# Dealing the rows of the first x tiles, meant to let a DMA engine read them in sequence

## The chip, the core and the metric

The kernel runs on one core of one Trainium2 chip. The metric is the device time of one execution in microseconds (us); medians of several executions are quoted. A ratio is the mean time of one kernel's runs over that of the other's of the same rounds, so it is not quite the ratio of the medians quoted beside it.

Engines: PE is TensorE, PEld its weight loads, DVE VectorE, ACT ScalarE, POOL GpSimd; SP only issues DMAs here ("SPq" is its queue).

## The reference

```python
B, S, Dm, Df = 1, 2048, 1024, 3584          # bf16 inputs
g = jnp.einsum("bsd,df->bsf", x, w_gate)
u = jnp.einsum("bsd,df->bsf", x, w_up)
h = gelu_tanh(g) * u
return jnp.einsum("bsf,fd->bsd", h, w_down)
```

## The kernel before

The kernel works in two passes (`ip`) of 1024 rows of x, each of two halves (`c`) of 512 rows, with a recursive matrix product that needs fewer multiplications. All of this is unchanged. What matters is the very beginning. The first 512 rows come as four tiles of 128 rows, are transposed by PE, and only then can the first product with the weights start. The other x blocks come by DMA transposes.

```python
    def store(ip, c, i, dc, put):
        st = slot([P, N], bf16, "st")
        put(st)
        r0 = (2 * ip + c) * N + i * P
        nc.sync.dma_start(out=out2[r0 : r0 + P, dc * N : (dc + 1) * N], in_=st)
    ...
    def load_x(c):
        t = []
        for i in range(NS):                       # four tiles, 256 KB each
            xn = slot([P, Dm], bf16, "xn")
            r0 = c * N + i * P
            nc.sync.dma_start(out=xn, in_=x2[r0 : r0 + P, :])
            t.append(xn)
        return t
    ...
    xT = new_x()
    xn0 = load_x(0)
    wf = wpool.tile([P, 2, NKB, 2 * P], bf16, name="w")
    for k0, k1 in ((0, 2), (2, 5), (5, NKB)):
        load_wf(nc.sync, k0, k1)                  # the first weights
    w = load_w(1)
    for ko in range(NKB):
        transposing(xT, 1, ko, N)                 # second half of x, by DMA transpose
    ...
        keep_warm(NWARM, N)
        for i in range(NS):
            if i == 2:
                keep_warm(2, 2 * P)
            turn(xT, xn0, 0, i)                   # PE transposes of tile i
        plain(bank[0:4], 0, range(0, 2), parts=2) # first products with weights
```

## Time and profile before

| what | value |
|---|---|
| time, median of 3 runs (6 by the time of the result) | 539.86 us (540.15) |
| lowest and highest of these 6 | 539.61, 540.94 |
| PE busy | 534.1 of 538.8 us |
| PE's last unbroken stretch | 7.91 to 535.68 us |
| last of the four x tiles landed | 6.99 us |

The page of the kernel before gives the span, the busy time of PE and the chain of work that ended last.

```profile
span 538.8 us, 7447 instructions
...
PE 534.1 (99%) x2409; PEld 381.2 (71%) x2409; DVE 341.5 (63%) x524; ACT 261.4 (49%) x463; POOL 238.5 (44%) x215
...
PE 98%; DMA 1%; SPq 0%; ACT 0%; issue 0%
```

The chain of waits in order of time, kernel before (start in us, length in us, what):

```profile
2.12 4.87 DMA xn<-in_x_dram
6.99 0.05 issue
7.04 0.62 PE bank L447 x8
7.66 0.22 PE bank L111 x2
7.88 0.03 issue
7.91 527.77 PE bank L111 x2366
```

From 7.91 to 535.68 us the chain is PE and nothing else; a last store of the output follows. Whatever starts that stretch earlier or later moves the end by the same amount, as long as nothing new makes PE wait. The 4.87 us of DMA ahead of it are the loads that the change touches.

The view of the tile `xn`, kernel before. The SPq line has the duration of one issue on SP (least, median, most, in ns); the last line is the time from issue to landing.

```profile
L440 SPq DMA_DIRECT2D xn<-in_x_dram x4: 392/420/432, 0.7 to 2.1; - x4
...
  PEld L447: 1.8, 3
...
DMA to landing us min/median/max: 2.8/3.8/4.9
```

The trace also records every DMA packet and, on the semaphore of each load, 16 completions, read here as one for each of the 16 DMA engines that the profile counts. The first x is 512 packets of 2 KB.

### The profile page before, as it was taken

The numbers are of one execution on the slowest core, as the hardware profiler recorded it, in microseconds if no ns is written. First come the engines' busy times: TensorE is split into PE (matmuls) and PEld (weight loads), VectorE is DVE, ScalarE is ACT, GpSimd is POOL, SyncE is SP. The second block draws the span as 40 slices with busy tenths as digits, with TensorE's granted clock in tenths as the row PEclk, the third lists the DMA queues.
The fourth block names the chain that finished last, engine by engine and source line by source line (L and its number), as shares of the span: only waits on it lengthen the run. The fifth ranks groups of instructions, "written<-read, shape, count | busy, mean of one in ns | idle before, by whom it ended". The sixth has DMA issues, their size and how long they took to land.

```text
span 538.8 us, 7447 instructions
## 1 busy us (share of the span) xinstructions
PE 534.1 (99%) x2409; PEld 381.2 (71%) x2409; DVE 341.5 (63%) x524; ACT 261.4 (49%) x463; POOL 238.5 (44%) x215
## 2 busy tenths in 40 slices
PE   8999999999999999999999999999999999999997
PEld 5568686867677746888867677676868685488886
DVE  2986766767676894694955455555554649676730
ACT  2556675766666410255355555555555551114431
POOL 1179966677773500000097767676766600000000
DMA  9675656749472999989872223242420049573751
GB/s 243 157 185 168 185 176 175 220 133 260 131 235 72 381 366 297 307 192 296 238 195 80 78 80 88 70 118 63 133 71 9 2 147 390 184 236 96 237 181 51
DMA packets 108198, 93.29 MB, mean 173 GB/s; under 512 B 17280, under 2 KB 93056, under 8 KB 108160
## 3 DMA queue, kind: packets, MB, share of 16 engines
q1 hardware_dynamic: 108160, 92.82, 59.4%
q8 instruction: 19, 0.31, 0.3%
q14 instruction: 19, 0.16, 0.1%
HBM read 74.45 MB, written 15.20 MB: 166 GB/s over the span
## 4 chain that ended last, share of the span: by engine, by line
PE 98%; DMA 1%; SPq 0%; ACT 0%; issue 0%
PE bank L111 98%; DMA xn<-in_x_dram 1%; SPq L440 0%; PE bank L447 0%; ACT st L412 0%
## 5 line engine op out<-in xcount | busy, mean ns | idle before, releaser
L93 POOL TENSOR_TENSOR s<-w 128x512 fp32r<-128x512 bf16 x102 | 119.2, 1189 | 163.2 <-DVE t L90 86.0
L111 PE MATMUL bank<-t,s 128*128 128x512 f32 x648 | 151.7, 390 | 0.0
L111 PEld LDWEIGHTS bank<-t,s 128*128 128x128 f32 x648 | 121.6, 188 | 25.5
L111 PE MATMUL bank<-xT,w 128*128 128x512 bf16 (+1 forms) x504 | 109.7, 376 | 0.0
L107 ACT COPY p<-bank 128x512 f32<-128x512 f32 x124 | 69.9, 590 | 45.4 <-PE bank L111 44.9
L111 PEld LDWEIGHTS <-w 128*128 128x128 bf16 x504 | 48.1, 98 | 58.1 <-issue 3.4
L90 DVE TENSOR_TENSOR hT<-g,bank 128x512 bf16<-128x512 f32 x112 | 76.8, 687 | 17.5 <-PE bank L111 4.5
L90 DVE TENSOR_TENSOR sum<-bank,p 128x512 f32<-128x512 f32 x54 | 37.3, 691 | 79.5 <-PE bank L111 78.4
L179 ACT ACTIVATE g<-sum 128x512 f32<-128x512 f32 x81 | 51.4, 635 | 74.5 <-DVE sum L90 74.2
L111 PE MATMUL bank<-q 128*128 128x512 f32 x240 | 58.9, 389 | 0.0
L93 POOL TENSOR_TENSOR s<-w,s 128x512 fp32r<-128x512 bf16 x50 | 57.7, 1176 | 0.0
L93 POOL TENSOR_TENSOR s<-s,w 128x512 fp32r<-128x512 f32 x50 | 57.2, 1165 | 0.0
L111 PE MATMUL bank<-t,sa 128*128 128x512 f32 x216 | 55.9, 401 | 0.0
L111 PE MATMUL bank<-tb,s 128*128 128x512 f32 x216 | 53.3, 389 | 0.0
L107 ACT COPY u<-bank 128x512 f32<-128x512 f32 x62 | 35.5, 589 | 33.5 <-PE bank L111 33.2
L111 PEld LDWEIGHTS bank<-q 128*128 128x128 f32 x240 | 45.0, 188 | 9.4
L111 PE MATMUL bank<-raw,hT 128*128 128x512 bf16 x224 | 48.7, 379 | 0.0
L102 ACT CAST tb<-raw 128x512 fp32r<-128x512 bf16 x28 | 17.3, 626 | 62.1 <-PE bank L111 27.6
L111 PEld LDWEIGHTS bank<-t,sa 128*128 128x128 f32 x216 | 40.6, 188 | 9.5
L111 PEld LDWEIGHTS bank<-tb,s 128*128 128x128 f32 x216 | 40.5, 188 | 8.4
L90 DVE TENSOR_TENSOR bank<-bank,p 128x512 f32<-128x512 f32 x54 | 37.7, 699 | 8.8 <-PE bank L111 6.2
L90 DVE TENSOR_TENSOR q<-hT 128x512 fp32r<-128x512 bf16 x56 | 38.4, 685 | 4.3 <-PE bank L111 4.3
(44 smaller groups left out, 442.1 us busy)
## 6 DMA issues: line engine op xcount, KB each, us to landing
raw<-in_w_down_dram SPq DMA_DIRECT2D x76, 256.0 KB, 5.0
q<-td SPq DMA_DIRECT2D x60, 256.0 KB, 5.1
w<-in_w_gate_dram SPq DMA_DIRECT2D x27, 512.0 KB, 5.9
w<-in_w_up_dram SPq DMA_DIRECT2D x27, 512.0 KB, 7.0
td<-m SPq DMA_DIRECT2D x12, 768.0 KB, 4.5
w<-td SPq DMA_DIRECT2D x6, 1024.0 KB, 10.0
out_dram<-st SPq DMA_DIRECT2D x32, 128.0 KB, 1.7
td<-w SPq DMA_DIRECT2D x2, 768.0 KB, 6.2
```

What stands on the lines that cost most here:

```text
L90: nc.vector.tensor_tensor(out=out, in0=a, in1=b, op=op)
L93: nc.gpsimd.tensor_tensor(out=out, in0=a, in1=b, op=op)
L102: nc.scalar.copy(out=t, in_=src)
L107: nc.scalar.copy(out=t, in_=ps)
L111: nc.tensor.matmul(ps, lhsT=lhs, rhs=rhs, start=start, stop=stop, skip_group_check=True)
L179: nc.scalar.activation(g, src, ACT.Gelu_apprx_tanh)
```

## The change

The intent: over the four tiles each DMA engine should read 64 KB in sequence, eight rows (16 KB) per tile, and not jump 256 KB from tile to tile. 64 KB is 1 MB in 16 equal shares. Row 32e + 8i + j goes to partition 8e + j of tile i. The columns of that half of x are then permuted through both products, and the stores of these rows put them back.

```diff
+    def dealt(rows, i):
+        return rows[:N].rearrange("(e i j) d -> i e j d", i=NS, j=8)[i]
+
     def store(ip, c, i, dc, put):
         st = slot([P, N], bf16, "st")
         put(st)
         r0 = (2 * ip + c) * N + i * P
-        nc.sync.dma_start(out=out2[r0 : r0 + P, dc * N : (dc + 1) * N], in_=st)
+        to = out2[:, dc * N : (dc + 1) * N]
+        to = dealt(to, i) if ip == c == 0 else to[r0 : r0 + P]
+        nc.sync.dma_start(out=to, in_=st)
 ...
             xn = slot([P, Dm], bf16, "xn")
-            r0 = c * N + i * P
-            nc.sync.dma_start(out=xn, in_=x2[r0 : r0 + P, :])
+            nc.sync.dma_start(out=xn, in_=dealt(x2, i))
```

## The prediction

> What bounds the kernel. The page's busy table has PE at 534.1 of 538.8 us (99%). The chain of work that ended last is 98% PE matmuls: from 7.91 us to 535.68 us it is PE without a break (527.77 us). Ahead stand 0.67 us of start, 1.45 us in which SP issues the four loads of the first x, 4.87 us of DMA until the last of them lands at 6.99 us, and 0.84 us of transposes and first matmuls. The change touches these 4.87 us, about 1% of the span, and eight of 32 output stores (128 KB, landing in 1.7 us by the DMA view), which nothing in the chain waits for.
>
> What the change does. Bytes, packets (2 KB rows) and issues stay the same. Before, each 256 KB tile is one contiguous stretch[...]. The columns of the c = 0 half are permuted consistently through both products and put back by the stores, so no engine computes more. I expect all 16 DMA engines still[...]. Issue cost stays about 0.42 us (the weight loads' more complex patterns take 0.43 to 0.49 us), at most 0.2 us more over four, hidden once data flow.
>
> What could be gained. In the packet records an undisturbed x packet of 2 KB takes 84 ns, for 16 engines 390 GB/s; 1 MB would take 2.7 us from the first packet at 1.76 us. It took 4.3 us for 15 engines (last completion but one at 6.05 us) and the sixteenth came at 6.99 us. Between 2.2 and 4.6 us some 25 packets take 0.2 to 0.7 us and one 1.50 us; that one is the straggler, and it holds back every later load on its engine by 0.94 us, also the weights that the first matmul waits for until 7.91 us. If the stalls come from jumps between tiles, they would go: 0.94 us from the straggler and, as an upper estimate, some 2.4 us if the loads ran undisturbed. The x landings also release SP's next issues (SP wait view), so a gain would be passed on to weights and DMA transposes. But the 0.7 us spread of the three runs before looks as if the stall is partly chance.[...]
>
> So I expect a small gain, some 0.4 us on average: 539.4 us, 80% range 538.2 to 540.5. Faster by over 2%: 0.5%; within 2%: 99%; slower: 0.5%.
>
> What would show it. Right: PE's unbroken stretch keeps its 527.8 us and starts between 6.5 and 8.0 us; the landing times of xn shrink from 2.8/3.8/4.9 us (min/median/max) to at most 2.8/3.5/4.2; fewer packets above 0.2 us before 4.6 us; the weight load's wait for xn falls below 1.8 us. Wrong: the stall packets stay as many (the jump was not their cause) and the time is unchanged; or landings exceed 5 us[...] and the time rises by up to 1 us; or a new PE gap opens near 23 us, where the DMA transposes land only some 0.4 us before their use; or fewer than 16 engines carry the load and landings grow several times.

The cut marks stand for statements that no trace or run of this case shows: how an engine reads a tile before and after, why 16 engines should stay in use, and why a distance of 64 KB should do no harm or how it could.

## More of the kernel before

Busy time of the engines in stretches of 2 us, kernel before (the last two columns are the DMA engines' share and GB/s):

```profile
2.00:4.00 2.00, 2.00 (x8) 0.83 (x7) 0.00 (x0) 0.01 (x1) 0.00 (x0) 1.00 1.01 297
4.00:6.00 2.00, 1.65 (x18) 1.36 (x15) 0.69 (x1) 0.54 (x1) 0.00 (x0) 1.00 0.98 322
6.00:8.00 2.00, 1.55 (x19) 1.10 (x20) 1.00 (x2) 1.76 (x2) 0.00 (x0) 1.00 1.14 306
```

The DMA engines are full from 2 us on (shares of 1.01 and 0.98 in the first two of these stretches). The start is therefore bound by when the first bytes come and by the rate at which they come.

## The result, and the profile after

The changed kernel took 541.31 us (median of 6 runs, 540.88 to 542.18), the kernel before 540.15 us (6 runs): ratio 1.0023, 95% interval 1.0010 to 1.0036. It became slower by about 1.2 us where a gain of about 0.4 us was predicted. In the profiled runs the span grew from 538.8 to 539.6 us.

The chain of waits in order of time, kernel after:

```profile
2.75 5.08 DMA xn<-in_x_dram
7.83 0.05 issue
7.88 0.62 PE bank L451 x8
8.50 527.88 PE bank L111 x2368
```

PE's stretch is as long as before (527.88 us; two more matmuls count into it), but it starts at 8.50 us. The loss is at the start alone: the chain's DMA piece begins 0.63 us later and lasts 0.21 us longer.

The view of the tile `xn`, kernel after:

```profile
L444 SPq DMA_DIRECT2D xn<-in_x_dram x4: 578/595/702, 0.7 to 2.8; - x4
...
  PEld L451: 3.0, 4
...
DMA to landing us min/median/max: 3.6/4.2/5.1
```

One issue on SP takes 0.60 us in place of 0.42, and the first, which nothing hides, 0.70 in place of 0.39. The weight loads are issued after the x loads on the same queue, so they slip as well: the first of them starts at 3.39 us in place of 2.60. The landings are later at every tile.

Busy time in stretches of 2 us, kernel after:

```profile
2.00:4.00 2.00, 1.92 (x5) 0.46 (x3) 0.00 (x0) 0.01 (x1) 0.00 (x0) 1.00 0.87 231
4.00:6.00 2.00, 1.61 (x17) 1.38 (x18) 0.54 (x1) 0.00 (x0) 0.00 (x0) 1.00 1.02 250
6.00:8.00 2.00, 1.06 (x14) 0.60 (x12) 0.84 (x2) 1.85 (x2) 0.00 (x0) 1.00 1.20 260
```

In the second of these stretches the DMA engines are as full as before (1.02 for 0.98) and move less: 250 for 322 GB/s. They are not short of work; the same packets take longer. The packet records say how:

| first x, 512 packets of 2 KB | before | after |
|---|---|---|
| first packet starts | 1.76 us | 2.23 us |
| packets of 80 to 90 ns | 442 | 201 |
| packets of 105 to 170 ns | 21 | 263 |
| packets over 200 ns | 22 | 24 |
| all packet times, summed, over 16 engines | 3.27 us | 4.05 us |
| middle engine (mean of the 8th and 9th of 16) done with the fourth tile, from the first packet | 3.87 us | 4.98 us |
| last engine done with the fourth tile, from the first packet | 5.23 us | 5.60 us |

So two things changed, the start (+0.47 us) and the duration of half of the packets. One thing did not: the packets over 200 ns, the stalls that the prediction hoped to remove, are as many as before. In the profiled run of before one of them held one engine back by 0.94 us, which hides part of the difference in the two profiled spans.

### The profile page after: what moved, and what is told of

Its sections match the earlier page's. It is cut to its first block, busy times and chain, and to the rows that moved or that the text cites. A ratio compares the mean times of both kernels' runs of the same rounds, so it can differ in the third digit from the quotient of the medians.

```text
span 539.6 us, 7447 instructions
## 1 busy us (share of the span) xinstructions
PE 534.2 (99%) x2409; PEld 380.8 (71%) x2409; DVE 341.3 (63%) x524; ACT 261.2 (48%) x463; POOL 238.6 (44%) x215
## 4 chain that ended last, share of the span: by engine, by line
PE 98%; DMA 1%; SPq 0%; ACT 0%; issue 0%
PE bank L111 98%; DMA xn<-in_x_dram 1%; SPq L444 0%; PE bank L451 0%; ACT st L417 0%
```

## The experiments

Three theories for the loss at the loads:

- **P, the pattern** (theory 1 and 2 in slow_path's expectation are its two halves). The source of a dealt load has three dimensions (16 groups of 8 rows of 1024) and no longer two. This makes the issue longer, and perhaps the packets too.
- **M, the memory.** Groups of rows that stand 64 KB apart, or a tile that is not one contiguous stretch, are served more slowly.
- **S, the shape**, formed after the first four runs. A source of 16 by 8 makes the packets slow, and one of 32 by 4 does not.

Each experiment ran in five or six timed runs, with 9 or 11 runs of the kernel before on the same chip; "loss" is the difference of the medians. The experiments ran in three sets of rounds, each on another chip: loads_only, row_deal, pitch18 and pitch66; then slow_path, deal_32x4, stride3 and stores_only; then groups4, pitch18_again, after_again and stride5. A comparison of losses from two sets is therefore also one between chips. Times of kernels whose loads do the same as before still differ by up to 0.4 us, so a loss is known to about that.

### loads_only: the loads of the change, the stores of before

```diff
-        to = dealt(to, i) if ip == c == 0 else to[r0 : r0 + P]
+        to = to[r0 : r0 + P]
```

> The four loads of the change, the stores as before (so 512 rows of the output come out in the wrong order, on purpose). Theory A, all of the loss is at the loads: the same time as the changed kernel, +1.0 to +1.4 us on before, PE's unbroken stretch 527.8 us, first matmul of the weights at 8.0 to 8.6 us. Rival, the stores cost something: at most +0.6 us.

541.47 us against 540.12: loss 1.35 us, ratio 1.0025 (1.0013 to 1.0038). 186 packets of 105 to 170 ns, first packet at 2.19 us, PE's stretch 527.83 us from 8.66 us on (just outside the expected 8.0 to 8.6). The output is wrong. The loads alone carry the whole loss.

### stores_only: the stores of the change, the loads of before

```diff
-            nc.sync.dma_start(out=xn, in_=dealt(x2, i))
+            r0 = c * N + i * P
+            nc.sync.dma_start(out=xn, in_=x2[r0 : r0 + P, :])
```

> Wrong result on purpose: loads of before, stores of the change. Theory A, nothing in the chain waits for stores: time as before within 0.3 us. Rival: up to +0.5 us, with a longer stretch of PE.

540.34 us against 539.92: 0.42 us, ratio 1.0006 (0.9994 to 1.0019), wrong output. This is a little outside what was expected and not clear of noise; its interval holds 1. PE's products took as long in the profiled run as before, 528.0 us from the first to the last, so the longer stretch that the rival asked for is not there. With loads_only, which lost as much as the full change without these stores, no cost of the stores is shown.

### row_deal: the same idea with a two-dimensional pattern

Partition p of tile i gets row 4p + i, in the loads and in the stores. The result is right.

```diff
-        return rows[:N].rearrange("(e i j) d -> i e j d", i=NS, j=8)[i]
+        return rows[:N].rearrange("(p i) d -> i p d", i=NS)[i]
```

> Right result. Partition p of tile i holds row 4p + i:[...] a tile takes every fourth row, and the source pattern has two dimensions as before. Theory P, the pattern with three dimensions costs the time (issue 0.58 to 0.70 us for 0.42, and slower packets): issue back to 0.42 us, first packet at 1.76 us, packets at 84 ns, time equal to before within 0.4 us. Theory M,[...] issue 0.42 us, first packet at 1.76 us, but median packet 110 to 140 ns and +0.5 to +0.9 us on before.

541.43 us against 540.12: loss 1.31 us, ratio 1.0020 (1.0006 to 1.0033). The issue is back at 0.42 us, the first packet at 1.75 us, and only 41 packets take 105 to 170 ns. Still the middle engine needs 4.97 us and not 3.87. Neither theory had this: the summed packet time is 3.27 us per engine, as before, so the time is lost between packets and not in them. Its profiled run also has a pause of PE of 0.22 us at 207.7 us, so not all of its loss need be at the start. stride3 and stride5 below look for the reason.

### pitch18 and pitch66: the pattern with other distances

The loads have the three-dimensional pattern of the change, but the groups of eight rows stand 9 rows (18 KB) or 33 rows (66 KB) apart and not 32. Results are wrong.

```diff
-            nc.sync.dma_start(out=xn, in_=dealt(x2, i))
+            r0 = i * 144                          # pitch66: i * 8
+            far = x2[r0 : r0 + 9 * 16].rearrange("(e j) d -> e j d", j=9)   # pitch66: 33, 33
+            nc.sync.dma_start(out=xn, in_=far[:, :8])
```

> Wrong result on purpose: the three-dimensional pattern of the change[...]. Theory P: issue 0.6 to 0.7 us, first packet at 2.2 us, median packet about 130 ns, +1.0 to +1.4 us on before. Theory M: issue and first packet as in P, but packets at 84 ns, so only the late start of +0.3 to +0.6 us is left.

> Wrong result on purpose: as the change[...]. Theory P: as the change, +1.0 to +1.4 us, packets about 130 ns. Theory M with a power of two at fault: packets back at 84 ns and +0.3 to +0.6 us. Theory M with mere distance at fault: packets about 130 ns, +1.0 to +1.4 us.

pitch18: 541.34 us, loss 1.22 us, 147 slow packets, middle engine 5.02 us. pitch66: 541.62 us, loss 1.50 us, 165 slow packets, middle engine 4.85 us. Both lose time as the change does, with nearly contiguous rows and with a distance that is no power of two. Theory P had the size of the packets wrong: their median stayed at 84 ns (about 115 in the change), since only about 30% became slow and not half. The same kernel as pitch18, run again below, has 241 slow packets, so this number varies from run to run. Theory M falls as the reason for the change's slow packets: they come with the pattern.

### slow_path: the kernel before, with one mark taken off its x loads

In the built program each of the four x loads of before carries a mark, `ant_dge_precooked`; the dealt loads do not have it. The library's switch takes it off without touching rows, partitions or dimensions. The result is right.

```diff
             r0 = c * N + i * P
+            nc.dge_precook = False
             nc.sync.dma_start(out=xn, in_=x2[r0 : r0 + P, :])
+            nc.dge_precook = True
```

> The kernel before with its own two-dimensional x loads, rows and partitions; only a mark that the program carries on each plain load[...] is taken off these four loads. Right result. Theory 1, the change lost that mark, and only that made the issue long: issue 0.58 to 0.70 us for 0.42, first packet at 2.2 us for 1.76, packets still at 84 ns, +0.3 to +0.7 us on before. Theory 2, unmarked loads also move slowly: packets around 110 to 133 ns and +1.0 to +1.4 us. Theory 3, the mark does nothing: issue 0.42 us, time as before.

540.60 us against 539.92: loss 0.68 us, ratio 1.0013 (1.0000 to 1.0025). All five runs lie above all nine of before (lowest 540.34, highest 540.24), though the interval of the ratio reaches down to 1.0000. The view of the tile `xn`, kernel slow_path:

```profile
L441 SPq DMA_DIRECT2D xn<-in_x_dram x4: 579/588/601, 0.7 to 2.6; - x4
```

The typical issue is as long as in the change, the first packet comes at 2.11 us, and the packets are as fast as before (18 slow ones; middle engine 3.69 us). This is theory 1 of its expectation. Losing the mark makes the issue long and the first packet late, by 0.34 us here, and does not slow the packets. The first issue takes 0.58 us, though, and 0.68 to 0.70 in every kernel whose loads have three dimensions without the mark: about 0.1 us of the first issue goes with the dimensions after all.

The chain of waits in order of time, kernel slow_path, shows where the late issues arrive:

```profile
2.64 0.60 SPq L441
3.28 3.88 DMA w<-in_w_gate_dram
7.16 0.05 issue
7.21 0.39 PE bank L111 x2
```

It runs through all four x issues to the first weight load, which starts 0.68 us later than in before (3.28 for 2.60 us). That load carries its mark in the built program, and its issue is long all the same, 0.60 us for 0.43; the next weight load is back at 0.46 us. So the loss of 0.68 us is as large as the delay of SP's queue, not as that of the first packet. This is read from one trace; no run tested it by itself. Nor do the two profiles show the loss directly: before's was a slow run (540.66 us) and this one the fastest of its five (540.34 us), and PE's long stretch starts at 7.91 us in the former and at 7.62 us in the latter. The loss rests on the timed runs.

### deal_32x4: 32 groups of four rows

```diff
-        return rows[:N].rearrange("(e i j) d -> i e j d", i=NS, j=8)[i]
+        return rows[:N].rearrange("(e i j) d -> i e j d", i=NS, j=4)[i]
```

> As the change, but 32 groups of four rows and not 16 groups of eight (row 16e + 4i + j): right result, pattern with three dimensions, unmarked.[...] Theory S,[...] with 32 by 4 the packets go back to 84 ns (median; few between 105 and 170 ns), and only the late start is left, +0.3 to +0.7 us. Rival M, the scattered rows in memory slow the packets: over 150 of 512 packets between 105 and 170 ns, +1.0 to +1.4 us.

540.94 us against 539.92: loss 1.02 us, ratio 1.0020 (1.0008 to 1.0033), right result. Only 9 packets take 105 to 170 ns, and the middle engine needs 3.97 us: the slow packets are gone with the shape. The time did not follow as far as theory S said (0.3 to 0.7 us). In the profiled run two stalls of over 1.5 us kept the last engines until 5.38 us after the first packet, but that is one run, and the loss is a median of five. So S had the packets right, and what the slow packets cost in time stays open.

### groups4 and pitch18_again: the closest pair

groups4 has 32 groups of four rows, 10 KB apart; pitch18 has 16 groups of eight, 18 KB apart. Both have three dimensions, no mark, and nearly contiguous rows, and both give wrong results. The diff is against pitch18.

```diff
-            r0 = i * 144
-            far = x2[r0 : r0 + 9 * 16].rearrange("(e j) d -> e j d", j=9)
-            nc.sync.dma_start(out=xn, in_=far[:, :8])
+            r0 = i * 160
+            far = x2[r0 : r0 + 5 * 32].rearrange("(e j) d -> e j d", j=5)
+            nc.sync.dma_start(out=xn, in_=far[:, :4])
```

> Wrong result on purpose. The pair of pitch18: unmarked three-dimensional x loads of nearly contiguous rows, but 32 groups of four rows, 10 KB apart (five rows, of which four are read), where pitch18 has 16 groups of eight, 18 KB apart. Theory S[...]: under 40 of 512 packets between 105 and 170 ns, the middle engine done with the fourth x about 3.7 to 4.0 us after the first packet, +0.5 to +0.9 us on before. Rival (unmarked plus any gap in memory is slow): 100 and more such packets, 4.8 us and more, +1.0 to +1.4 us as pitch18.

> The same kernel as pitch18, in the rounds of groups4. Theory S: as the first time, 100 and more packets between 105 and 170 ns, 4.8 to 5.2 us for the middle engine, and 0.3 to 0.7 us longer than groups4. Rival: no difference to groups4 beyond 0.2 us.

groups4: 541.03 us against 540.16, loss 0.87 us, ratio 1.0013 (1.0001 to 1.0025), 17 slow packets, middle engine 4.22 us. pitch18_again: 541.27 us, loss 1.11 us, ratio 1.0026 (1.0010 to 1.0041), 241 slow packets, middle engine 4.62 us. The slow packets follow the shape of 16 by 8 as theory S says. In time the pair lies 0.24 us apart by the medians and 0.0013 (0.7 us) by the ratios, which one run of pitch18_again at 543.61 us pulls apart. The intervals overlap, so only the sign is likely. Three numbers fell between the theories: the middle engine of groups4 (S had 3.7 to 4.0 us, the rival 4.8 and more), that of pitch18_again (S had 4.8 to 5.2 us), and the difference in time (S had 0.3 to 0.7 us, the rival at most 0.2).

The view of the tile `xn`, kernel groups4:

```profile
L446 SPq DMA_DIRECT2D xn<-in_x_dram x4: 582/603/691, 0.7 to 2.8; - x4
```

and kernel pitch18_again:

```profile
L446 SPq DMA_DIRECT2D xn<-in_x_dram x4: 573/598/693, 0.7 to 2.7; - x4
```

The issues are equally long in both, so the shape of the groups makes no difference on SP. What differs is in the transfer.

### after_again: the changed kernel in the same rounds

> The changed kernel again, beside groups4 and pitch18. All theories: +1.0 to +1.4 us on before. If the distance in memory (64 KB) costs something by itself, it is over 0.3 us longer than pitch18; if not, within 0.3 us of it.

There is no edit. 541.38 us against 540.16: loss 1.22 us, ratio 1.0020 (1.0008 to 1.0032), 232 slow packets, middle engine 5.15 us. This is within 0.3 us of pitch18_again, so no separate cost of the 64 KB distance is shown.

### stride3 and stride5: why row_deal was slow

These are the kernel before with two-dimensional, marked loads of every third row (6 KB apart) or every fifth row (10 KB), where row_deal takes every fourth (8 KB). Results are wrong.

```diff
-            r0 = c * N + i * P
-            nc.sync.dma_start(out=xn, in_=x2[r0 : r0 + P, :])
+            far = x2[: 5 * P].rearrange("(p five) d -> p five d", five=5)   # stride3: three; tile 3 starts at row 3 * P
+            nc.sync.dma_start(out=xn, in_=far[:, i])
```

> Wrong result on purpose: the kernel before, but its x loads take every third row (6 KB apart), marked, two dimensions. It asks why row_deal (every fourth row, 8 KB apart) lost 1.1 us with marked loads. Theory A,[...] with 6 KB last x landing but one at 6.0 to 6.4 us, time as before within 0.4 us. Theory B, any scatter of 2 KB rows costs: landing at 7 to 7.5 us as in row_deal, +0.8 to +1.4 us.

> Wrong result on purpose: row_deal with five in place of four, so tile i takes rows 5p + i (10 KB apart and not 8 KB), marked, two dimensions. Theory A, the power-of-two stride made row_deal slow: middle engine done in 3.9 to 4.3 us and +0.2 to +0.6 us on before, as stride3. Theory B, wide strides cost: nearer to row_deal, 4.8 us and more, +0.9 us and more.

stride3: 540.37 us against 539.92, loss 0.45 us, ratio 1.0008 (0.9994 to 1.0022), middle engine 4.18 us. Theory A blames the power of two among the distances, theory B any scatter of rows. The last engine but one of stride3 was done at 6.79 us, later than theory A had it, while the time held roughly. stride5: 540.44 us against 540.16, loss 0.28 us, ratio 1.0003 (0.9990 to 1.0016), middle engine 4.01 us. Scattered rows at 6 and 10 KB cost little; at 8 KB they cost 1.31 us. That the power of two is the slow distance fits all three, but only three distances were tried, and why it should be slow was not shown.

### All in one table

"Slow" counts packets of 105 to 170 ns, "stalls" those over 200 ns, of 512. "Middle engine" (the mean of the eighth and ninth of 16 completions) and "last engine" are times from the first packet to the completion of the fourth tile. All but the loss is from the one profiled run.

| kernel | source pattern, marked | first packet, us | slow | stalls | middle engine, us | last engine, us | loss, us |
|---|---|---|---|---|---|---|---|
| before | 128 rows, yes | 1.76 | 21 | 22 | 3.87 | 5.23 | 0 |
| stores_only | 128 rows, yes | 1.76 | 23 | 25 | 3.95 | 4.92 | 0.42 |
| stride5 | 128, every 5th, yes | 1.79 | 14 | 18 | 4.01 | 4.71 | 0.28 |
| stride3 | 128, every 3rd, yes | 1.76 | 8 | 27 | 4.18 | 5.04 | 0.45 |
| row_deal | 128, every 4th, yes | 1.75 | 41 | 19 | 4.97 | 5.74 | 1.31 |
| slow_path | 128 rows, no | 2.11 | 18 | 28 | 3.69 | 4.26 | 0.68 |
| groups4 | 32 x 4, no | 2.20 | 17 | 22 | 4.22 | 5.69 | 0.87 |
| deal_32x4 | 32 x 4, no | 2.19 | 9 | 31 | 3.97 | 5.38 | 1.02 |
| pitch18 | 16 x 8, no | 2.20 | 147 | 32 | 5.02 | 5.63 | 1.22 |
| pitch18_again | 16 x 8, no | 2.21 | 241 | 20 | 4.62 | 5.42 | 1.11 |
| pitch66 | 16 x 8, no | 2.20 | 165 | 28 | 4.85 | 5.67 | 1.50 |
| loads_only | 16 x 8, no | 2.19 | 186 | 23 | 4.51 | 5.80 | 1.35 |
| after | 16 x 8, no | 2.23 | 263 | 24 | 4.98 | 5.60 | 1.16 |
| after_again | 16 x 8, no | 2.25 | 232 | 23 | 5.15 | 5.68 | 1.22 |

The stores differ too: stores_only, pitch18, pitch66, groups4, pitch18_again and after_again have those of the change, row_deal and deal_32x4 have stores dealt as their loads, and the others have those of before.

The column of slow packets splits cleanly: 147 to 263 with 16 by 8, at most 41 with everything else. The first packet splits cleanly too: 1.75 to 1.79 us with the mark, 2.11 to 2.25 without it.

One thing the medians leave out: three of the 32 runs with 16 by 8 show a granted clock of only 0.996 or 0.997 and are the slowest of their kernels (loads_only 542.55, pitch66 542.54, pitch18_again 543.61 us); none of the 29 runs of before beside the experiments is under 0.999. The profile of pitch66 is such a run: the clock granted to PE is 0.73 from 6 to 8 us and 0.50 from 8 to 10 us, and eight transposes take 1.03 us in place of 0.62. What brings this on was not tested.

## Why the prediction was wrong

**What held.** The engine at the limit and the place of the change on the critical path were right: PE's stretch kept its length (527.77 and 527.88 us), no PE gap opened later, and what the start lost came out at the end. The change stayed far within 2%. The 16 engines all carried the load as far as the trace shows it: each x load has 16 completions, in the changed kernel none earlier than 1.55 us after the first packet.

**The step that failed first: "Issue cost stays about 0.42 us", "at most 0.2 us more over four, hidden once data flow".** It took 0.60 us, and 0.70 for the first, 0.8 us more over four (2.62 for 1.82). The first issue is not hidden: no data flow before it. The first packet came 0.47 us later, and the weight loads behind came 0.79 us later. The sign was there: the prediction's own first paragraph has 1.45 us of SP issues on the chain, ahead of the DMA. The comparison with the weight loads, which have three dimensions and took 0.43 to 0.49 us in five of the first six, misled, because the number of dimensions was not what counts most. Those loads carry the mark in the built program, the dealt loads do not, and slow_path shows that losing the mark alone makes 0.42 into 0.59 us; its time rose by 0.68 us, known to about 0.4.

**The second step that failed, and with it the gain: "If the stalls come from jumps between tiles, they would go".** They did not. Packets over 200 ns number 18 to 32 in every kernel of the table, whatever its layout, and 24 in the changed one. One sign was there in advance: the prediction itself noted that the spread of the runs looked like chance. What causes the stalls stays open. No experiment moved them.

**Third: the split over the engines, on which the change rests, was assumed.** The author took it that an engine reads 16 KB of a tile in a row and then jumps to the next tile. The trace does not name the engine of a packet, so no run here shows this, and the kernel before may never have read in that way. What the runs show is that the shape of the source counts: 147 to 263 slow packets with 16 by 8, and 9 and 17 with 32 groups of four. Why the shape makes the packets slow was not shown. It may change which rows an engine reads, in what order, or where it writes them, and no run changes one of these and holds the others still.

**The sum.** Without the mark the loss is 0.68 to 1.02 us (slow_path, groups4, deal_32x4; mean 0.86); with 16 by 8 as well it is 1.11 to 1.50 us (six sets of runs; mean 1.26). So most of the 1.2 us, 0.7 to 0.9, seems to go with the late issues, and an estimated 0.4 us is left for the slow packets. This second share is not clear of noise: in the rounds that groups4, pitch18_again and after_again had in common it is 0.24 and 0.35 us, with losses known to about 0.4. The first share is larger than the 0.34 to 0.47 us by which the first packet is late, but fits the 0.68 to 0.79 us by which SP gets to the weight loads later (slow_path and after). In the profiles the slow packets delay the middle engine by 0.6 to 1.2 us (4.51 to 5.15 us, against 3.96 us, the mean of slow_path, groups4 and deal_32x4), but the first product waits for the last engine, which the stalls hold back in any case; that is a likely reason why less of it arrives in the time.

**The 64 KB distance** did no harm by itself that these runs could show: pitch18 at 18 KB lost 1.22 us, as much as the change. The prediction had "landings exceed 5 us" among the signs that it was wrong, and they did reach 5.1 us, but so they did at 18 KB. The intended gain was not found in any version either: the groups of deal_32x4 carry on from tile to tile as well, four rows each, with fast packets, and it is still 1.02 us slower than before. No experiment beat the kernel before.

## What to carry to other kernels

Ahead of this kernel's first work the DMA issues were exposed, and not only the first of them, so check that a changed access pattern keeps its issue duration and the start of its first packet before counting on better transfers. A new row order can change more than addresses. Here a source with 128 leading rows kept the mark and the short issue (0.42 us), 32 groups of four kept only the fast packets (9 and 17 slow ones, issue 0.60 us), and 16 groups of eight kept neither (147 to 263 slow ones, 0.60 us); but row_deal kept both and still lost 1.31 us, so none of this alone makes an order safe. And if a stall is to be removed by a new layout, first check by a second trace that the stall belongs to the layout; here it was in every layout (18 to 32 packets of 512).
